# Sixteen loads of V moved from SyncE's queue to ScalarE's

## The chip, the cores and the metric

The kernel runs on one core of one Trainium2 chip. The core has five engines with an instruction stream each: TensorE (PE, matmuls; PEld is its weight load), VectorE (DVE), ScalarE (ACT), GpSimd (POOL) and SyncE (SP, which computes nothing and issues transfers). They meet only at semaphores. The metric is the device time of one execution in microseconds.

## The reference

One transformer layer over 2048 positions of width 512: a modulated layer norm, attention with 32 heads of 16 in which each position looks at itself and seven earlier positions at a distance of 2, 4, ... 14, the output projection, then a second modulated layer norm and a gated feed-forward of width 1792. Cut to what matters here:

```
qkv = h @ wqkv                                  # h = layernorm(x) * (1 + ca) + sa
idx = pos[:, None] - 2 * arange(8)[None, :]     # masked where idx < 0
logits = einsum('bhsd,bhswd->bhsw', q, k[idx]) * Dh ** -0.5
o = einsum('bhsw,bhswd->bhsd', softmax(logits), v[idx])
x = x + ga * (o @ wo)
out = x + gb * ((silu(h2 @ w1) * (h2 @ w3)) @ w2)   # h2 = layernorm(x) * (1 + cb) + sb
```

## The kernel before

The 2048 positions are sixteen tiles T of 128. Everything is bf16 except the sums in PSUM. Per tile the attention goes like this. VectorE multiplies Q with eight shifted views of K (line 706), TensorE sums the products per head into logits (line 716), VectorE and ScalarE make the softmax (lines 728 to 769, the exponential on line 746). For the values, each tile of V is copied out of PSUM by ScalarE (line 685) and stored to a scratch array in device memory (`v_scratch_dram`, line 689). Later the function `values` loads a shifted window of it back: 128 rows of 6144 bytes, 768 KB, from the tile itself and from the end of the one before it (line 776). That is **the V load**, one per tile. VectorE multiplies what it brought with the attention weights (line 783, below: the V product), TensorE sums (line 792), ScalarE copies the sum out (line 798), a transposing transfer turns it (line 799), TensorE applies the output projection (line 804), VectorE adds the residual (line 808). The feed-forward runs in five groups of tiles: gate and up projections on TensorE (line 820), Silu (line 826) and the copy of the up half (line 830) on ScalarE, their product on VectorE (line 831), the down projection (lines 851 and 863), the residual (line 879), the store of the output (line 881).

Nothing of this order is found at run time. `_build` makes some 1100 operations; a list `ORDER` written out in the file places them in one sequence, and each engine's program is that sequence with the other engines' operations left out. `synchronize` then gives each operation the waits that it needs and that its own engine has not already passed. A transfer is an operation of the engine that issues it: it stands in that engine's program, its waits are waited for there, and everything later in that program stands behind it. Before the change all transfers but the load of `c` are in SyncE's program.

A V load waits for the store of its tile's V (for even tiles also of the tile before; tile 0 for the zero padding instead) and for the V product that last used its buffer. There are three buffers: two of `vsh`, and `vshx`, which lies over weights that are dead by then. `SLOTS` names the buffer for each load.

The places of the V loads in `ORDER` beside ScalarE's operations, with the times of the profiled execution (us from the start of the span; the last instruction of ScalarE ahead of the load in the list, the first behind it):

| tile | buffer | SyncE issues | lands | ScalarE ahead | ScalarE behind | V product starts |
|---|---|---|---|---|---|---|
| 0 | vsh 0 | 30.20 | 35.36 | L665 26.30-26.71 | L612 28.76 | 43.99 |
| 1 | vsh 1 | 30.85 | 37.26 | L612 29.44-30.21 | L524 30.10 | 41.79 |
| 2 | vsh 0 | 51.14 | 56.93 | L685 48.79-49.41 | L665 49.27 | 65.80 |
| 3 | vsh 1 | 53.47 | 61.95 | L664 57.64-58.24 | L685 58.84 | 62.76 |
| 4 | vsh 1 | 65.07 | 70.12 | L826 66.92-67.30 | L665 67.20 | 79.71 |
| 5 | vsh 0 | 73.81 | 78.99 | L826 78.47-78.86 | L830 79.00 | 83.58 |
| 6 | vshx | 76.64 | 82.33 | L569 83.09-83.91 | L798 83.81 | 96.31 |
| 7 | vsh 0 | 87.01 | 92.09 | L612 87.13-87.73 | L826 87.58 | 93.39 |
| 9 | vsh 1 | 90.08 | 95.18 | L826 95.96-96.34 | (tile 12's load) | 132.31 |
| 12 | vsh 0 | 95.71 | 100.32 | (tile 9's load) | L830 96.25 | 161.74 |
| 8 | vshx | 120.68 | 126.16 | L826 129.88-130.48 | L826 130.37 | 130.10 |
| 10 | vshx | 132.42 | 137.25 | L830 131.80-132.44 | L830 133.56 | 139.72 |
| 11 | vsh 1 | 134.62 | 140.98 | L798 136.41-137.03 | L830 137.67 | 142.26 |
| 15 | vshx | 142.04 | 146.73 | L826 142.93-143.53 | L830 143.72 | 171.96 |
| 13 | vsh 1 | 148.41 | 152.72 | L830 150.88-151.48 | L830 151.35 | 164.55 |
| 14 | vsh 0 | 164.04 | 169.88 | L798 175.75-176.34 | L798 176.24 | 175.82 |

Of the kernel before, what the change touches and what calls it, by code (L numbers as in the profile page):

```python
# [260 lines left out]
def c_act(n):  # L261
    return 66 + n * 107 // 128


def c_dve(n):
    return 60 + n * 137 // 128
# [12 lines left out]
def _build(p, A_x, A_wqkv, A_wo, B_w1, B_w3, B_w2, c, w_mod, out):  # L279
# [68 lines left out]
    def bank(v):  # L348
        return PALL[:, v.at * 512:(v.at + 1) * 512]
# [52 lines left out]
    vkpad, vzrow, vvpad = Val("kpad"), Val("zrow"), Val("vpad")  # L402
# [18 lines left out]
    for i in range(3):  # L421
        for half in range(2):
            p.dma(wqkv[:, half::2, i * D:(i + 1) * D], wqkv_view[:, half::2, i * D:(i + 1) * D], ("load", 3 + i), (256, 1024),
                  w=[vwq[i][half]])
# [22 lines left out]
    for g in range(NG):  # L447
# [8 lines left out]
         r=[vthc, vcT], w=[vc4])  # L456
# [3 lines left out]
         r=[vc4, vident] + wm_hold, w=[vpc])  # L460
# [169 lines left out]
    vq, vk, vv_dram = {}, {}, {}  # L630
# [142 lines left out]
    def values(T, i, val):  # L773

        vv = Val("vsh", vshpool)
        p.dma(lambda: vv.at[:], bass.AP(v_dram, (PAD + T * P - 2) * D, [[4 * D, 32], [-4 * D, 4], [1, 6 * D]]), ("vl", T), (128, 6144),
              r=[vv_dram[T]] + ([] if T % 2 else [vv_dram[T - 1]] if T else [vvpad]), w=[vv], cost=640, again=True)
        vr = Val("pr", pqpool)

        def av(e):  # L780
            a_w = bass.AP(val.at, i * 8 * H, [[2 * 8 * H, P], [H, 8], [0, DH], [1, H]])
            v_w = bass.AP(vv.at, 2 * D, [[6 * D, P], [-2 * D, 2], [D, 4], [1, D]])
            return e.tensor_tensor(bass.AP(vr.at, 0, [[8 * D, P], [1, 8 * D]]), v_w, a_w, ALU.mult)  # L783

        avs[T] = p.op("dve", av, C_PQ, ("av", T), r=[val, vv], w=[vr], lock=True)
        vo, vt = Val("ps_o", psum), Val("ot", otpool)

        def acc(e):
            b = bank(vo)
            for wf in range(2):  # L790
                for c in range(4):
                    ins = e.matmul(b[32 * c:32 * c + 32, :], ind[:], bass.AP(vr.at, (4 * wf + c) * D, [[8 * D, P], [1, D]]),  # L792
                                   start=(wf == 0), stop=(wf == 1), tile_position=(0, 32 * c))
            return ins

        p.op("pe", acc, C_RED, ("ac", T), r=[vr, vind], w=[vo], tiled=True)
        va = Val("oa", oapool)
        p.op("act", lambda e: e.activation(va.at[:], bank(vo), ACT.Copy), c_act(512), ("ac", T), r=[vo], w=[va])  # L798
        p.dma(lambda: vt.at[:], lambda: va.at[:], ("ac", T), (128, 1024), r=[va], w=[vt], cost=1250, transpose=True)
        vy = Val("ps_y", psum)  # L800

        def wop(e):
            for ft in range(KT):
                ins = e.matmul(bank(vy), vt.at[:, ft, :], wo[:, ft, :], start=(ft == 0), stop=(ft == KT - 1))  # L804
            return ins

        p.op("pe", wop, 4 * MM, ("wo", T), r=[vt, vsc_wo], w=[vy])
        p.op("dve", lambda e: e.scalar_tensor_tensor(x_sb[:, T, :], bank(vy), 1.0, x_sb[:, T, :], op0=ALU.mult, op1=ALU.add,  # L808
                                                     accum_out=sx[:, T, :]), c_dve(512) + 12, ("rs", T), r=[vy], w=[vx[T], vsx[T]])
# [103 lines left out]
    for groups in BLOCKS:  # L913
        vls = [logits(Ts) for Ts in groups]
        ves = [shift(Ts, vl) for Ts, vl in zip(groups, vls)]
        for Ts, vl, ve, vx_ in zip(groups, vls, ves, exps(groups, vls, ves)):
            val = softmax(Ts, vl, ve, vx_)
            for i, T in enumerate(Ts):
                values(T, i, val)
# [102 lines left out]
```

## Time and profile before

| | us, or as said |
|---|---|
| time of the runs shown, median (lowest, highest) | 246.49 (245.53, 247.45) |
| the profiled execution's own time | 247.83 |
| its span, first to last instruction | 245.8 |
| granted TensorE clock, mean (no time, share of full) | 0.992 |
| moved by SyncE's queue (q1) | 35.94 MB |
| moved by ScalarE's queue (q10) | the 1 KB load of `c` |

Busy is the time in which an engine executes an instruction; issuing a transfer is not counted. The idle time that the views show before an instruction is put down to whatever released it last. A row of the timeline is: start, duration, engine (SPq and ACTq are the issuing parts of SyncE and ScalarE), line, operation, tiles, how many were merged, and in brackets the idle time before it with its releaser. All transfers carry line 127, that of the helper that issues them.

### The profile page before, as it was taken

To read this page: it belongs to the slowest core of one execution; us is meant where nothing else is said; L and a number is where in the kernel's file an instruction comes from. 1 tells how busy PE (TensorE), PEld (TensorE's weight loads), DVE (VectorE), ACT (ScalarE), POOL (GpSimd) and SP (SyncE) were. 2 spreads that over 40 slices of the span, in tenths; PEclk is the share of its full clock that TensorE was granted. 3 is DMA by queue.
4 is the path that set the end of the run, shared out by engine and by line. 5 is a ranking of instruction groups with operands and counts; after the bars stand their busy time and mean duration, and the time that the engine had idled before them with its cause. 6 is when DMAs were issued, how large, how long until landed. Compare 5 with 4: busy or idle time off the path is not lost.

```text
span 245.8 us, 4285 instructions
## 1 busy us (share of the span) xinstructions
PE 234.7 (96%) x1669; PEld 120.1 (49%) x1669; DVE 173.1 (70%) x305; ACT 154.5 (63%) x305; POOL 20.9 (8%) x52
## 2 busy tenths in 40 slices
PE   7799999999998999899899999999999999999994
PEld 2557555444556666545443434443334444444473
DVE  4567999999897899988999996592942322142621
ACT  2168677797998889764587879456556944351200
POOL 4124111002000200031000001100000110000000
PEclk9799999999999999999999999999999999999999
DMA  6999979879958687703332964443031120010002
GB/s 191 345 311 350 303 273 207 188 185 350 299 131 249 217 214 244 173 21 67 87 126 59 266 164 154 72 109 121 21 87 23 43 65 16 9 57 9 3 19 67
DMA packets 39348, 36.21 MB, mean 147 GB/s; under 512 B 18832, under 2 KB 36256, under 8 KB 39328
## 3 DMA queue, kind: packets, MB, share of 16 engines
q1 hardware_dynamic: 39320, 35.94, 51.6%
q8 instruction: 13, 0.21, 0.4%
q14 instruction: 7, 0.06, 0.1%
q10 hardware_dynamic: 8, 0.00, 0.0%
HBM read 27.53 MB, written 4.21 MB: 129 GB/s over the span
## 4 chain that ended last, share of the span: by engine, by line
PE 48%; DMA 3%; ACT 2%; DVE 0%; issue 0%; DVEq 0%
PE pall L820 30%; PE pall L863 12%; PE pall L804 3%; DMA sb_h<-sb_xn 2%; PE pall L792 2%; DMA out_dram<-sb_o 1%; ACT sb_h L589 1%; PE pall L851 1%; DVE sb_o L879 0%; ACT sb_xn L569 0%; PE pall L716 0%; ACT sb_hh L830 0%; DVEq L225 0%
## 5 line engine op out<-in xcount | busy, mean ns | idle before, releaser
L820 PE MATMUL pall<-sb_h,sb_w 128*128 128x512 bf16 (+1 forms) x560 | 101.5, 337 | 1.4 <-ACT sb_h L589 1.0
L820 PEld LDWEIGHTS pall<-sb_h,sb_w 128*128 128x128 bf16 x560 | 51.5, 98 | 50.4 <-ACT sb_sg L826 5.8
L826 ACT ACTIVATE sb_sg<-pall 128x512 bf16<-128x512 f32 (+1 forms) x70 | 34.0, 514 | 26.5 <-PE pall L820 25.9
L863 PE MATMUL pall<-sb_w,sb_hh 128*128 128x512 bf16 x196 | 43.5, 379 | 0.0
L706 DVE TENSOR_TENSOR sb_pq<-sb_q,sb_kT 128x4096 bf16<-128x4096 bf16 x16 | 36.3, 2282 | 0.0
L656 PE MATMUL pall<-sb_h,sb_wqkv 128*128 128x512 bf16 (+1 forms) x160 | 33.0, 350 | 1.0 <-DVE sb_h L619 0.6
L830 ACT ACTIVATE sb_hh<-pall 128x256 bf16<-128x256 f32 (+1 forms) x56 | 26.3, 493 | 9.6 <-PE pall L820 9.0
L863 PEld LDWEIGHTS pall<-sb_w,sb_hh 128*128 128x128 bf16 x196 | 19.0, 98 | 22.8 <-DVE sb_hh L831 0.3
L783 DVE TENSOR_TENSOR sb_pq<-sb_vsh,sb_al 128x4096 bf16<-128x4096 bf16 x12 | 27.3, 2286 | 1.1 <-PE pall L716 0.8
L831 DVE TENSOR_TENSOR sb_hh<-sb_sg,sb_hh 128x256 bf16<-128x256 bf16 (+1 forms) x56 | 18.5, 352 | 11.7 <-ACT sb_hh L830 11.3
L879 DVE TENSOR_TENSOR sb_o<-pall,sb_x 128x512 bf16<-128x512 f32 (+1 forms) x18 | 11.0, 628 | 16.8 <-PE pall L863 12.4
L656 PEld LDWEIGHTS pall<-sb_h,sb_wqkv 128*128 128x128 bf16 x160 | 15.0, 102 | 15.2 <-ACT sb_v L685 1.2
L834 DVE TENSOR_TENSOR sb_hh<-sb_sg,pall 128x512 bf16<-128x512 bf16 x14 | 8.9, 684 | 15.3 <-PE pall L820 13.2
L804 PE MATMUL pall<-sb_wo,sb_ot 128*128 128x512 bf16 x64 | 16.0, 379 | 2.6 <-DMA sb_ot<-sb_oa 2.5
L589 ACT ACTIVATE sb_h<-sb_h,sb_modc 128x512 bf16<-128x512 bf16 x16 | 11.7, 811 | 10.0 <-DMA sb_h<-sb_xn 10.0
L612 ACT ACTIVATE sb_h<-pall,sb_modc 128x256 bf16<-128x256 bf16 (+1 forms) x22 | 12.5, 649 | 8.4 <-DVE sb_modc L487 6.1
L564 POOL TENSOR_SCALAR sb_rs<-sb_var 128x2 f32<-128x2 f32 x8 | 4.0, 500 | 147.7 <-ACT sb_xn L558 147.7
L675 PE MATMUL pall<-sb_wqkv,sb_h 128*128 128x512 bf16 x64 | 16.5, 379 | 0.0
L808 DVE SCALAR_TENSOR_TENSOR sb_x<-pall,sb_x 128x512 bf16<-128x512 f32 x16 | 10.9, 688 | 8.0 <-PE pall L804 7.9
L569 ACT ACTIVATE sb_xn<-sb_x,sb_nb,sb_rs 128x512 bf16<-128x512 bf16 x16 | 12.5, 809 | 4.4 <-DVE sb_nb L566 4.4
L665 ACT ACTIVATE sb_kT<-pall 128x512 bf16<-128x512 f32 (+1 forms) x20 | 9.9, 521 | 4.9 <-PE pall L656 4.7
L558 ACT ACTIVATE sb_xn<-sb_x,sb_nm 128x512 bf16<-128x512 bf16 x16 | 11.4, 713 | 2.3 <-DVE sb_nm L554 2.2
(79 smaller groups left out, 217.1 us busy)
## 6 DMA issues: line engine op xcount, KB each, us to landing
sb_vsh<-v_scratch_dram SPq DMA_DIRECT2D x12, 768.0 KB, 5.2
sb_w<-in_B_w_dram SPq DMA_DIRECT2D x6, 512.0 KB, 6.7
sb_vshx<-v_scratch_dram SPq DMA_DIRECT2D x4, 768.0 KB, 5.2
sb_x<-in_A_x_dram SPq DMA_DIRECT2D x18, 128.0 KB, 5.1
sb_w<-in_B_w_dram SPq DMA_DIRECT2D x6, 384.0 KB, 8.2
v_scratch_dram<-sb_v SPq DMA_DIRECT2D x16, 128.0 KB, 5.6
out_dram<-sb_o SPq DMA_DIRECT2D x14, 128.0 KB
sb_wqkv<-in_A_wqkv_dram SPq DMA_DIRECT2D x6, 256.0 KB, 6.4
```

Of the source, the lines that this page charges most:

```text
L569: p.op("act", lambda e, vn=vn, T=T: e.activation(vn.at[:], x_sb[:, T, :], ACT.Identity, bias=nb[:, T, :], scale=rs[:, NT + T, :]), c_act(5 ...
L589: return e.activation(vh.at[:, ft, 0:n * P], vh.at[:, ft, 0:n * P], ACT.Identity, bias=modc[:, 8 * which + ft:8 * which + ft + 1], scale=m ...
L656: ins = e.matmul(bank(vp)[:, 0:n], wqkv[:, t, kind * D + ft * P:kind * D + (ft + 1) * P], vh.at[:, t, 0:n], start=(t == ORDER[0]), stop=(t ...
L675: ins = e.matmul(bank(vp), vh.at[:, t, tt * P:(tt + 1) * P], wqkv[:, t, 2 * D:3 * D], start=(t == ORDER[0]), stop=(t == ORDER[-1]))
L706: return e.tensor_tensor(vp.at[:], in0, in1, ALU.mult)
L783: return e.tensor_tensor(bass.AP(vr.at, 0, [[8 * D, P], [1, 8 * D]]), v_w, a_w, ALU.mult)
L804: ins = e.matmul(bank(vy), vt.at[:, ft, :], wo[:, ft, :], start=(ft == 0), stop=(ft == KT - 1))
L820: ins = e.matmul(bank(vp)[:, 0:n], wt[:, t, fi * P:(fi + 1) * P], vh.at[:, t, 0:n], start=(t == 0), stop=(t == KT - 1))
L826: p.op("act", lambda e: e.activation(vt.at[:, 0:n], bank(vgp)[:, 0:n], ACT.Silu), c_act(n), k, r=[vgp], w=[vt], table="silu")
L830: p.op("act", lambda e: e.activation(vh_.at[:, 0:n], bank(vup)[:, 0:n], ACT.Copy), c_act(n), k, r=[vup], w=[vh_])
L831: p.op("dve", lambda e: e.tensor_tensor(vh_.at[:, 0:n], vt.at[:, 0:n], vh_.at[:, 0:n], ALU.mult), 60 + n * 69 // 128, k, r=[vt], w=[vh_], ...
L863: ins = e.matmul(bank(vz), vhh[fi].at[:, tt * P:(tt + 1) * P], w2[:, fi, :], start=(fi == 0), stop=(fi == NF - 1))
```

## The change

The V load gets the argument `eng="act"`. The helper `dma` hands it to `op`, which puts the operation into that engine's program. `ORDER` and `SLOTS` stay as they are, so each V load takes the place in ScalarE's program that the table above shows, with the waits that ScalarE has not passed by then. The stores of V, the transposing transfers, the weights, x and the output stay with SyncE, in their order.

```diff
@@ -774,7 +774,7 @@
         vv = Val("vsh", vshpool)
         p.dma(lambda: vv.at[:], bass.AP(v_dram, (PAD + T * P - 2) * D, [[4 * D, 32], [-4 * D, 4], [1, 6 * D]]), ("vl", T), (128, 6144),
-              r=[vv_dram[T]] + ([] if T % 2 else [vv_dram[T - 1]] if T else [vvpad]), w=[vv], cost=640, again=True)
+              r=[vv_dram[T]] + ([] if T % 2 else [vv_dram[T - 1]] if T else [vvpad]), w=[vv], cost=640, again=True, eng="act")
```

## The prediction

> **What bounds the kernel now.** I read the page's busy times first, then the chain of work that ended last in order of time.
>
> ```profile
> span 245.8 us, 4285 instructions
> PE 234.7 (96%) x1669; PEld 120.1 (49%) x1669; DVE 173.1 (70%) x305; ACT 154.5 (63%) x305; POOL 20.9 (8%) x52
> ```
> ```profile
> 121.05 14.21 PE pall L820 x64
> ...
> 205.83 24.17 PE pall L820 x112
> ```
>
> TensorE is busy 96% of the span, and from 121 us to the last tiles the chain runs along its matmuls alone. A wait that TensorE gets is therefore paid in full, and a wait that goes pays only if TensorE stood behind it. So the second question is who waits for V loads now. In the view of waits the V product (L783) is never held by a transfer; the first row below is its only one, for a matmul. The largest of TensorE's waits for transfers is for the transposed attention output, which stays where it is:
>
> ```profile
> DVE sb_pq L783 <- PE pall L716: 0.8, 1, 0.8
> ...
> PE pall L804 <- DMA sb_ot<-sb_oa: 2.5, 3, 1.3
> ```
>
> SyncE, on the other hand, waits for V products before it can issue V loads into used buffers:
>
> ```profile
> SPq L127 <- DVE sb_pq L783: 20.8, 6, 10.5
> ```
>
> These 20.8 us leave SyncE. Nothing is late because of them: if every wait of TensorE for a transposed tile vanished too, 2.5 us were gained, 1%. So the change has little to win, and the question is what it costs on ScalarE.
>
> **The change part by part.** Per load three things move: the issue itself, the waits ahead of it, and the moment of issue, which becomes ScalarE's place in the list instead of SyncE's.
>
> The issue costs this on SyncE (minimum, median, maximum in ns), and the one transfer that ScalarE issues today costs it the same there:
>
> ```profile
> L127 SPq DMA_DIRECT2D sb_vsh<-v_scratch_dram x12: 518/586/617, 30.2 to 164.0; - x12
> DMA to landing us min/median/max: 4.3/5.2/8.5
> ```
> ```profile
> 0.78 0.55 ACTq L127 DMA_DIRECT2D sb_c<-in_c_dram  x1
> ```
>
> Sixteen times 0.59 us are 9.4 us of ScalarE's queue. How much of that the engine feels depends on whether its queue gets ahead of it. The trace shows that it does. The semaphore waits of the activation on L589 start at 112.4, while the activation before it in the program starts only at 113.31:
>
> ```profile
> L225 ACTq EVENT_SEMAPHORE  x2: 17/1406/2795, 112.4 to 112.5; - x2
> ```
> ```profile
> 113.31 0.83 ACT L569 ACTIVATE sb_xn<-sb_x,sb_nb,sb_rs 128x512 bf16<-128x512 bf16 x1
> ```
>
> So I take it that a V load is issued as soon as the activation ahead of it has its semaphores, some 0.5 to 2 us before that activation ends, and that an issue of 0.59 us is hidden wherever ScalarE has an activation running and one queued. That covers tiles 1, 2, 4, 5, 6, 7, 11, 13 and 15; I put 0.2 us on the nine together, with 4.4 us as the upper end (six fully paid at 0.59, two that a short gap follows at 0.4, tile 11 in a gap of 0.65). Tiles 9 and 12 stand back to back, 1.2 us of issue against one short activation: 0.4 us, between 0 and 0.9.
>
> *Tile 0: a wait in front of the projections.* SyncE finishes an issue at 23.62 + 1.96 = 25.58 and then stands until 30.20, when the store of V's first tile has landed. That wait moves to ScalarE:
>
> ```profile
> 23.62 1.96 SPq L127 DMA_DIRECT2D sb_x<-in_A_x_dram  x4
> 30.20 1.25 SPq L127 DMA_DIRECT2D sb_vsh<-v_scratch_dram  x2
> ```
> ```profile
> 26.30 0.41 ACT L665 ACTIVATE sb_kT<-pall 128x256 bf16<-128x256 f32 x1
> 28.76 1.45 ACT L612 ACTIVATE sb_h<-pall,sb_modc 128x512 bf16<-128x512 bf16 x2 [2.05 <-PE pall L604]
> ...
> 32.05 0.59 ACT L664 ACTIVATE sb_q<-pall 128x512 bf16<-128x512 f32 x1
> ```
> ```profile
> 33.20 1.59 PE L716 MATMUL pall<-sb_pq,sb_E 128*32 128x256 bf16 x48
> ```
> ```profile
> 34.56 0.67 DVE L728 TENSOR_REDUCE sb_mx<-pall 128x64 f32<-128x512 f32 x1
> ```
> ```profile
> 30.00:40.00 10.00, 10.00 (x120) 5.33 (x119) 10.00 (x16) 7.84 (x15) 1.85 (x4) 1.00 0.81 270
> ```
>
> Queued behind it on ScalarE are the modulated transposes (L612) and the evacuations of the projections. They start at 30.20 + 0.59 = 30.8 instead of 28.76, 2.0 us late. TensorE's next projections want their banks and their input, the logits of 33.20 come 2.0 us late, and the row maximum of 34.56, which follows their end at once, 1.9 us. In 30 to 40 us TensorE and VectorE are both busy 10.00 of 10, so nothing there gives it back: **1.9 us**.
>
> *Tile 3: a later landing.* Its place on ScalarE is behind the activation of 57.64:
>
> ```profile
> 53.47 0.62 SPq L127 DMA_DIRECT2D sb_vsh<-v_scratch_dram  x1
> ```
> ```profile
> 57.64 0.60 ACT L664 ACTIVATE sb_q<-pall 128x512 bf16<-128x512 f32 x1 [0.48 <-PE pall L656]
> 58.84 0.60 ACT L685 ACTIVATE sb_v<-pall 128x512 bf16<-128x512 f32 x1 [0.60 <-DMA v_scratch_dram<-sb_v]
> ```
> ```profile
> 62.76 2.28 DVE L783 TENSOR_TENSOR sb_pq<-sb_vsh,sb_al 128x4096 bf16<-128x4096 bf16 x1
> 65.80 2.29 DVE L783 TENSOR_TENSOR sb_pq<-sb_vsh,sb_al 128x4096 bf16<-128x4096 bf16 x1 [0.75 <-PE pall L716]
> ```
>
> The issue itself fits into the 0.60 us before 58.84. With the median of 5.2 us it lands at 57.7 + 5.2 = 62.9, with the longest of 8.5 us at 66.2; the product starts at 62.76, and the idle 0.75 us behind it absorb as much. That is 0 to 2.7 us; I take 0.3, nearer the median, since the 8.5 us was a load queued behind weights in SyncE's own queue.
>
> *Tile 8: the place is too late.* SyncE issued this load 10 us before its product; on ScalarE it stands behind the first of the two activations of 129.88.
>
> ```profile
> 120.68 0.56 SPq L127 DMA_DIRECT2D sb_vshx<-v_scratch_dram  x1
> ```
> ```profile
> L225 ACTq EVENT_SEMAPHORE  x1: 17/17/17, 129.2 to 129.2; - x1
> ```
> ```profile
> 127.48 0.58 ACT L746 ACTIVATE pall<-pall 128x512 f32<-128x512 f32 x1
> ...
> 129.88 1.08 ACT L826 ACTIVATE sb_sg<-pall 128x512 bf16<-128x512 f32 x2
> ...
> 133.56 0.60 ACT L830 ACTIVATE sb_hh<-pall 128x512 bf16<-128x512 f32 x1 [1.13 <-PE pall L820]
> ```
> ```profile
> 130.10 2.29 DVE L783 TENSOR_TENSOR sb_pq<-sb_vshx,sb_al 128x4096 bf16<-128x4096 bf16 x1
> 132.31 2.28 DVE L783 TENSOR_TENSOR sb_pq<-sb_vsh,sb_al 128x4096 bf16<-128x4096 bf16 x1
> 134.51 0.75 DVE L831 TENSOR_TENSOR sb_hh<-sb_sg,sb_hh 128x512 bf16<-128x512 bf16 x2
> ```
> ```profile
> 135.18 1.05 PE L792 MATMUL pall<-sb_pq,sb_ind 128*32 128x512 bf16 x16
> ```
>
> The semaphore row is the wait of the second of those activations, so the queue has passed the V load's place by 129.2; it cannot be there much before the exponential starts at 127.48, with three instructions then waiting in front. I take 127.9. Landing 5.0 us later, 132.9, makes the product 2.8 us late (1.5 to 4.8 over issue from 127.3 to 129.2 and landings of 4.3 to 5.7). Two chains carry this to TensorE. VectorE's next product, of 132.31, ends 2.8 us late, and the sums of 135.18 follow it directly, with some 0.5 us between. And tile 10's load, next in ScalarE's queue, waits for tile 8's product to leave the shared buffer: ScalarE stands until 130.10 + 2.8 + 2.29 = 135.2, issues, and the copy of 133.56, for which TensorE needs the bank, starts at 135.8, 2.2 us late. Tile 10's and 11's products come after the shift and are not late a second time. **2.4 us** (1.0 to 4.3).
>
> *Tile 14: the place is too late again.* It stands between the two copies of 175.75:
>
> ```profile
> 164.04 0.58 SPq L127 DMA_DIRECT2D sb_vsh<-v_scratch_dram  x1
> ```
> ```profile
> 175.75 1.09 ACT L798 ACTIVATE sb_oa<-pall 128x512 bf16<-128x512 f32 x2 [0.34 <-PE pall L792]
> ...
> 181.04 0.60 ACT L826 ACTIVATE sb_sg<-pall 128x512 bf16<-128x512 f32 x1 [0.27 <-PE pall L820]
> ```
> ```profile
> 175.82 2.29 DVE L783 TENSOR_TENSOR sb_pq<-sb_vsh,sb_al 128x4096 bf16<-128x4096 bf16 x1 [0.30 <-PE pall L792]
> 179.08 0.43 DVE L831 TENSOR_TENSOR sb_hh<-sb_sg,sb_hh 128x512 bf16<-128x512 bf16 x1 [0.97 <-ACT sb_hh L830]
> ```
> ```profile
> 180.84 1.89 PE L804 MATMUL pall<-sb_wo,sb_ot 128*128 128x512 bf16 x8
> ```
>
> The first copy waited for a matmul, so the queue is not ahead here. Issue at 175.8, landing 5.2 us later at 181.0, product until 183.3, the gate product of 179.08 until 183.7; it frees the buffer that the Silu of 181.04 writes, which ends at 184.3 and frees the bank of the second output projection. That one started half-way through the row of 180.84, at 181.7: about **2.5 us**, 1.7 to 3.2 over landings of 4.3 to 5.8.
>
> On SyncE, behind the longest of the waits (10.5 us, for tile 10's load) stood a store of the output, which nothing awaits; on TensorE and VectorE no instruction changes. The sum is 1.9 + 0.3 + 0.4 + 2.4 + 2.5 + 0.2 = 7.7 us. The profiled execution took 247.83 us by its own time (span 245.8), so it would take 255.5. It lies 1.3 us above the median of the runs, 246.49; on the median the sum gives 254.2. With its bounds not all at one end the case spans 251 to 258.
>
> **The rivals.**
>
> *The queue gets further ahead, and the change is not slower by more than 2%.* If a V load need not wait until the activations ahead of it have their semaphores, tile 14's is issued while its copy still waits for TensorE. Landing by 178.3 costs nothing, by the 2.5 us just found, so it decides whether the issue comes before 173.1; tile 8's would be issued by 127.3 and cost 1.2 us. Left are 1.9 + 1.2 + 0.3, together 3.4: 249.9 us. For it speaks the lead at 112.4. Against it, the wait row of 129.2 came just after a VectorE result. [...]
>
> *The issue waits until ScalarE has finished what is ahead of it.* Then nothing is hidden: 4.4 for the nine, 0.9 for the pair, 0.8 for tile 3, 1.9 for tile 0; tile 8 issued at 130.48 lands 5.4 us late, 4.9 us for TensorE; tile 14 issued at 176.3 costs 3.1. Sum 16.0: 262.5 us. The lead in the trace speaks against it, but that row is a wait and no transfer.
>
> *The freed queue of SyncE makes it faster.* It would have to bring the transposed tiles sooner; their waits hold 2.5 us in all, and no V load is queued just ahead of them: at best 244, and only if ScalarE's waits cost nothing. [...]
>
> **How the numbers follow.** What a measurement of this kernel can tell from no change is about 2%, 4.9 us: 241.6 to 251.4. The forecast has 0.58, the early issue 0.22, the late issue 0.14, the gain 0.03; 0.03 is for slowdowns that I did not find. The forecast lies above 251.4 but for its lowest twentieth, the late issue wholly, the early issue mostly below. Slower: 0.55 + 0.14 + 0.03 = 0.72; faster by over 2%: 0.02; within: 0.26. The range takes in the early issue's value and the forecast's upper end and part of the way to the late issue: 249.3 to 259.8.
>
> **What would show it.** ScalarE idle before L612 near 28.8 until 30.8, with the idle put to a transfer; V products near 130 and 176 waiting for `sb_vshx` and `sb_vsh` transfers, 2 to 4 and 5 us; ScalarE idle until tile 8's product ends; issues on ACTq of 0.5 to 0.6 us that overlap running activations. If the V loads of tiles 8 and 14 are issued by 126 and 173, or only after the activation ahead has ended, the rule for the issue was wrong; if the products wait but the chain at the end is not longer, the cover was.

## The result

| | time, us (median; lowest to highest) | runs | against the kernel before |
|---|---|---|---|
| before | 246.49; 245.53 to 247.45 | 2 | |
| V loads on ScalarE | 261.98; 261.38 to 262.57 | 2 | 1.063, 95% interval 1.042 to 1.083 |

15.5 us were added where the prediction said 7.7, and the time lies outside its range. The profiled execution of the changed kernel took 262.57 us (span 260.5, 14.7 more than before), at the same mean granted clock, 0.992. Times of one kernel spread (256.03 to 261.26 us in e0_again below, at mean clocks of 1.000 and 0.985 to 0.987), because stretches at half clock, which are shown below, came and went from run to run, and the ratios leave out a run that is over 1.5% above the fastest of its kernel.

The page of the changed kernel: ScalarE and VectorE do the same work as before, TensorE's share falls from 96% to 91%, and two slices of the granted clock in the middle are no longer full.

```profile
PE 236.9 (91%) x1669; PEld 121.1 (46%) x1669; DVE 173.1 (66%) x305; ACT 154.7 (59%) x305; POOL 20.5 (8%) x52
...
PEclk9999999999999988999999999999999999999999
...
q10 hardware_dynamic: 2312, 12.58, 14.7%
```

The view of waits (who waited for whom: total, times, longest one) has four rows that were small or absent before. The first was 2.5 us; it is the one that the prediction called "the largest of TensorE's waits for transfers" and left out of the sum:

```profile
PE pall L804 <- DMA sb_ot<-sb_oa: 8.4, 5, 2.5
DVE sb_pq L783 <- DMA sb_vsh<-v_scratch_dram: 7.6, 3, 5.0
ACT sb_h L612 <- DMA v_scratch_dram<-sb_v: 5.8, 1, 5.8
...
DVE sb_pq L783 <- DMA sb_vshx<-v_scratch_dram: 1.9, 1, 1.9
```

**Where the time came in.** Taking the start of the same TensorE instruction in both records and noting where the difference jumps gives this account:

| place in the changed kernel's record | us added | what TensorE waited for |
|---|---|---|
| start, to 13 us | -1.2 | nothing; before was at half clock here |
| projection at 32.82 | 3.5 | ScalarE, which waited for the store of V's first tile |
| output projection of tile 1, 56.20 | 2.8 | transposed attention output |
| tile 5 | 0.8 | its V load landing late |
| output projection of tile 4, 95.42 | 2.4 | transposed attention output |
| 96.0 to 99.4 | 1.6 | nothing: half clock |
| tiles 9 and 12 | 0.5 | the pair of issues |
| between 57 and 92 and between 108 and 133 | 0.7 | several small ones |
| tile 8 | 1.3 | its V load landing late, and tile 10's load behind it |
| output projections of tiles 13 and 15, near 195 | 2.4 | transposed output, and tile 14's late load |

The sum is 14.8 us, against 14.7 between the spans. Some half of it, 7.6 us, stands in four rows to which the prediction gave nothing: the output projections of tiles 1 and 4, the landing of tile 5's load, the half clock.

**ScalarE at the first load.** The timeline of ScalarE and its issuing part (start, duration, engine, line, operation; in brackets the idle time before it and its releaser), and of TensorE:

```profile
30.67 0.60 ACTq L127 DMA_DIRECT2D sb_vsh<-v_scratch_dram  x1
31.32 0.78 ACT L612 ACTIVATE sb_h<-pall,sb_modc 128x512 bf16<-128x512 bf16 x1 [5.81 <-DMA v_scratch_dram<-sb_v]
31.37 0.55 ACTq L127 DMA_DIRECT2D sb_vsh<-v_scratch_dram  x1
32.00 0.77 ACT L612 ACTIVATE sb_h<-pall,sb_modc 128x512 bf16<-128x512 bf16 x1
```
```profile
32.82 1.04 PE L656 MATMUL pall<-sb_h,sb_wqkv 128*128 128x512 bf16 x4 [3.35 <-ACT sb_h L612]
```

The wait is where it was forecast, and it ends where it was forecast (30.7 plus the issue). But it is 5.8 us long, where the times of the forecast make 4.1 (26.7 to 30.8): ScalarE was through with its work ahead of it at 25.5. The second load, whose place is behind the activation of 32.00, was issued at 31.37: the issue ran 0.63 us ahead of the engine here.

**The transposed output.** Tile 2's load stands on ScalarE just ahead of the moment at which SyncE issues the transposing transfers of tiles 1 and 0:

```profile
50.21 0.52 ACTq L127 DMA_DIRECT2D sb_vsh<-v_scratch_dram  x1
```
```profile
50.39 2.61 SPq L127 DMA_TRANSPOSE sb_ot<-sb_oa  x2
```
```profile
56.20 1.04 PE L804 MATMUL pall<-sb_wo,sb_ot 128*128 128x512 bf16 x4 [2.49 <-DMA sb_ot<-sb_oa]
```

The view of transfers says what these two took from issue to landing (median of the two): the first row is from the record of before, the second from that of after.

```profile
sb_ot<-sb_oa SPq DMA_TRANSPOSE x2, 2.3
```
```profile
sb_ot<-sb_oa SPq DMA_TRANSPOSE x2, 5.4
```

And the packets of the 16 transfer engines in two stretches of the changed record, 51.6 to 54.4 and 54.4 to 56.0 us:

```profile
DMA packets 100, 0.61 MB, mean 219 GB/s; under 512 B 0, under 2 KB 0, under 8 KB 100
...
q10 hardware_dynamic: 100, 0.61, 83.8%
```
```profile
DMA packets 1114, 0.40 MB, mean 248 GB/s; under 512 B 1085, under 2 KB 1093, under 8 KB 1114
...
q1 hardware_dynamic: 1077, 0.27, 98.9%
```

The transposing transfers' packets are the small ones: 1085 of the 1114 of the second stretch are under 512 bytes. Issued at 50.4 and 51.7, these transfers have none in the first stretch: there only the 6144-byte rows of the V load run, 0.61 MB in 2.8 us, at 83.8% of the engines' time. When most of these are through, the small packets come in a dense block, SyncE's queue at 98.9%. So the two queues did not share the engines evenly in these stretches: of these transfers the one begun first was finished first.

### The profile page after: what moved, and what is told of

The parts are those of the page before. It is cut to its first block, busy times and chain, and to the rows that moved or that the text cites. A ratio compares the mean times of both kernels' runs of the same rounds, so it can differ in the third digit from the quotient of the medians.

```text
span 260.5 us, 4279 instructions
## 1 busy us (share of the span) xinstructions
PE 236.9 (91%) x1669; PEld 121.1 (46%) x1669; DVE 173.1 (66%) x305; ACT 154.7 (59%) x305; POOL 20.5 (8%) x52
## 3 DMA queue, kind: packets, MB, share of 16 engines
q10 hardware_dynamic: 2312, 12.58, 14.7%
## 4 chain that ended last, share of the span: by engine, by line
PE 40%; DMA 6%; ACT 3%; DVE 2%; issue 1%; ACTq 0%; DVEq 0%
PE pall L820 23%; PE pall L863 12%; PE pall L804 2%; DMA sb_vsh<-v_scratch_dram 2%; DMA sb_h<-sb_xn 2%; DMA sb_vshx<-v_scratch_dram 2%; DMA out_dram<-sb_o 1%; PE pall L792 1%; ACT sb_h L589 1%; DVE sb_pq L783 1%; PE pall L851 1%; ACT L746 0%; ACT sb_sg L826 0%; ACT sb_hh L830 0%; DVE sb_o L879 0%
## 5 line engine op out<-in xcount | busy, mean ns | idle before, releaser
L820 PE MATMUL pall<-sb_h,sb_w 128*128 128x512 bf16 (+1 forms) x560 | 103.1, 340 | 3.4 <-ACT sb_hh L830 1.5
L820 PEld LDWEIGHTS pall<-sb_h,sb_w 128*128 128x128 bf16 x560 | 52.5, 99 | 53.3 <-ACT sb_sg L826 5.5
L656 PE MATMUL pall<-sb_h,sb_wqkv 128*128 128x512 bf16 (+1 forms) x160 | 31.9, 341 | 3.9 <-ACT sb_h L612 3.7
L783 DVE TENSOR_TENSOR sb_pq<-sb_vsh,sb_al 128x4096 bf16<-128x4096 bf16 x12 | 27.3, 2287 | 7.6 <-DMA sb_vsh<-v_scratch_dram 7.6
L612 ACT ACTIVATE sb_h<-pall,sb_modc 128x256 bf16<-128x256 bf16 (+1 forms) x22 | 12.5, 651 | 11.9 <-DVE sb_modc L487 5.9
L834 DVE TENSOR_TENSOR sb_hh<-sb_sg,pall 128x512 bf16<-128x512 bf16 x14 | 8.9, 684 | 15.3 <-PE pall L820 13.2
L804 PEld LDWEIGHTS pall<-sb_wo,sb_ot 128*128 128x128 bf16 x64 | 5.4, 97 | 18.6 <-issue 6.7
L664 ACT ACTIVATE sb_q<-pall 128x512 bf16<-128x512 f32 (+1 forms) x20 | 9.7, 519 | 6.1 <-PE pall L656 6.1
## 6 DMA issues: line engine op xcount, KB each, us to landing
sb_wqkv<-in_A_wqkv_dram SPq DMA_DIRECT2D x6, 256.0 KB, 5.3
```

The lines of the kernel that those rows point to most:

```text
L656: ins = e.matmul(bank(vp)[:, 0:n], wqkv[:, t, kind * D + ft * P:kind * D + (ft + 1) * P], vh.at[:, t, 0:n], start=(t == ORDER[0]), stop=(t ...
L820: ins = e.matmul(bank(vp)[:, 0:n], wt[:, t, fi * P:(fi + 1) * P], vh.at[:, t, 0:n], start=(t == 0), stop=(t == KT - 1))
```

## The experiments

In kernels that have one line more, the lines of the views are larger by one (L783 is L784 there). The times are medians of all runs of a kernel. Each comparison is with runs of the kernel before on the same chip: 244.90 us (e0 to e3), 245.62 (e4 to e7), 245.14 (g), 246.72 (h).

| run | V loads on ScalarE | us | against before (95%) |
|---|---|---|---|
| e0_again | all | 260.22 (256.03 to 261.26) | 1.063, of the medians; 1.045 for the run of 256.03 |
| e1 | all but 0, 1 | 252.75 | 1.031 (1.026 to 1.035) |
| e2 | all but 2, 6 | 261.81 | 1.066 (1.057 to 1.074) |
| e3 | all but 8, 14 | 256.40 | 1.043 (1.035 to 1.050) |
| e4 | none, two places moved | 245.91 | 1.002 (0.999 to 1.004) |
| e5 | all, eleven at other places | 250.39 | 1.014 (1.008 to 1.021) |
| e6 | all, three in halves | 263.68 | 1.072 (1.067 to 1.078) |
| e7 | 4, 9 to 13, 15 | 245.38 | 0.999 (0.996 to 1.001) |
| g1 | e7's and 0, 1 | 253.47 | 1.033 (1.026 to 1.039) |
| g2 | e7's and 2, 6 | 251.19 | 1.023 (1.017 to 1.029) |
| g3 | e7's and 8, 14 | 251.04 | 1.019 (1.010 to 1.028) |
| g4 | all, idle time of TensorE filled | 263.47 | 1.067 (1.055 to 1.080) |
| h1 | all, nine at other places | 247.24 | 1.004 (1.000 to 1.007) |
| h2 | all but 2 to 7 | 256.35 | 1.041 (1.037 to 1.046) |
| h3 | e7's and 3, 5, 7 | 251.09 | 1.019 (1.011 to 1.026) |

For e1 to e3, e7, g1 to g3, h2 and h3 the edit to the kernel before is this, with the tiles of the table:

```diff
+ACT_V = (2, 3, 4, 5, 6, 7, 8, 9, 10, 11, 12, 13, 14, 15)
...
-              r=[...], w=[vv], cost=640, again=True)
+              r=[...], w=[vv], cost=640, again=True, eng="act" if T in ACT_V else "sp")
```

### The changed kernel again, and its groups taken back

> The changed kernel once more, for a tight interval. All theories: 261 to 263 us, 1.06 times the kernel before (246.49 us). What the trace should repeat, by the theory of the landings: ScalarE idle some 5.8 us before the activation of L612 near 31 us; the transposed attention output of tiles 1 and 4 landing 5.0 to 5.8 us after its issue instead of 2.3 to 2.4; a stretch of about 3 us at half the granted clock near 96 us. If the stretch at half clock or the late landings are missing in this profile at the same time, they were an accident of the first record.

260.22 us, and the waits repeat: ScalarE idle 4.6 us for the store of V ahead of L612, the transposed output of tiles 1 and 0 at 4.9 us (median), tile 4's at 5.6. The stretch at half clock did not repeat at 96 us; such stretches came at the start and behind the wait for tile 0. Of the four runs three had a mean clock of 0.985 to 0.987 and took 260.18 to 261.26 us, and the fourth had 1.000 and took 256.03. So in these runs some 4 us of the 15 are clock, and 11 are waits. The share differs from record to record: in the account of the first one, half clock adds 1.6 us and its absence at the start takes 1.2 off.

> V loads of tiles 0 and 1 back on SyncE, the other fourteen on ScalarE. Theory of the landings: ScalarE no longer waits 5.8 us for the store of V's first tile before L612, so the shift of TensorE near 30 us (3.5 us, net 2.3 against the clock of the start) goes: 2.3 to 3.5 us less than the changed kernel, 258.5 to 259.7 us. Rival, ScalarE pays for each issue (0.59 us): two issues less, 1.2 us, 260.8 us. Rival, two queues cost as such: 14 of 16 loads still there, 260 us and the wait at L612 is not what matters.

252.75 us, 7.5 less than e0_again: more than any theory gave. The store of V holds ScalarE no longer, and the clock stays full in three of the four runs (0.999 to 1.000). But the 7.5 us are not all the cost of tiles 0 and 1. Between the two profiled records 2.4 us are gained ahead of the place, where e0_again happened to be at half clock; 2.5 us are gained at the wait, 1.7 at half clock behind it and 1.5 at tile 4's output projection. At full clock the kernels differ by 3.5 us (256.03, one run, and a median of 252.52), nearly twice the 1.9 us of the prediction.

> V loads of tiles 2 and 6 back on SyncE, the other fourteen on ScalarE. Theory of the landings: the transposing transfers of the attention output of tiles 1 and 4 are no longer behind a load of 768 KB in the transfer engines and land 2.3 to 2.4 us after their issue again; TensorE's waits at L804 near 53 and 92 us go (2.8 and 2.4 us), and with the second of them the stretch at half clock (1.5 us): 6.7 us less, 255.3 us (256.8 if the stretch has another cause). Rival, each issue on ScalarE costs 0.59 us: 1.2 us less, 260.8 us. Rival, two queues cost as such: 2 of 16 parts of 15.5 us, 1.9 us less, 260 us.

261.81 us: nothing gained, though the mechanism did what was expected. TensorE's waits at the output projection fell from 8.4 to 1.8 us, and the transfers of tiles 1 and 0 landed after 2.3 us. Something took all of it back. The timeline has it:

```profile
70.99 4.49 DVE L784 TENSOR_TENSOR sb_pq<-sb_vsh,sb_al 128x4096 bf16<-128x4096 bf16 x2 [3.76 <-DMA sb_vsh<-v_scratch_dram]
```
```profile
73.88 0.60 ACT L666 ACTIVATE sb_kT<-pall 128x512 bf16<-128x512 f32 x1 [1.97 <-DVE sb_pq L784]
```

Tile 3's load, issued on ScalarE at 62.04, now finds ahead of it the weights and x that SyncE issued behind tile 2's load, and lands 8.9 us later. The packets from 62.0 to 62.6 us are all SyncE's, 207 of the 231 between 512 bytes and 2 KB:

```profile
DMA packets 231, 0.21 MB, mean 353 GB/s; under 512 B 24, under 2 KB 231, under 8 KB 231
...
q1 hardware_dynamic: 231, 0.21, 104.6%
```

Tile 14's load in the changed kernel, with no packet of any queue between its issue and its first row, had that row 1.3 us after the issue (188.28 to 189.60) and landed after 4.8 us. Why the rows of SyncE's queue held up tile 3's load for so long stays open.

The product of tile 3 is 3.8 us late, and tile 4's load, which wants the same buffer, holds up ScalarE until that product ends, in front of an evacuation for TensorE.

> V loads of tiles 8 and 14 back on SyncE, the other fourteen on ScalarE. Theory of the landings: the products of tiles 8 and 14 are no longer late, and the transposed attention output of tile 13 is not behind tile 14's load: 1.3 and 2.4 us less, 258.3 us. The prediction on record put 2.4 and 2.5 us on them: 257.1 us. Rival, each issue on ScalarE costs 0.59 us: 1.2 us less, 260.8 us. Rival, two queues cost as such: 1.9 us less, 260 us.

256.40 us, 3.8 less than e0_again. The clock of these runs was lower (0.978 to 0.993), so the times alone would not settle it; the profiled records do. Against e0_again's TensorE gains 1.1 us at tile 8 and 2.4 us at the output projections near 195, 3.4 together, close to the 3.7 of the theory of the landings; the prediction's 4.9 was too high. The reverse, g3 against e7 below, shows 1.5 and 2.2 at the same places.

### The order without the queue

```diff
 ORDER = [
 ...
-    ... 272, 404, 405, ... 438, 422,
+    ... 272, 404, 422, 405, ... 438,
 ...
-    ... 345, 478, 668, ... 707, 454,
+    ... 345, 668, ... 707, 478, 454,
```

(422 and 478 are the V loads of tiles 2 and 6, 405 and 454 the transposing transfers of tiles 1 and 4; all on SyncE.)

> The kernel before, every transfer in SyncE's queue; only the places of the V loads of tiles 2 and 6 in the order are moved, to directly ahead of the transposing transfers of the attention output of tiles 1 and 4. Theory of the landings (a transfer issued just behind a load of 768 KB lands late, whichever queue it is in): TensorE waits 2.4 to 2.8 us longer at L804 at both places, 5 us together, up to 6.6 if a stretch at half clock follows the second: 251.5 to 253 us. Rival, two queues contend and one queue does not: 246.5 us.

1.002, no difference: the expectation of 5 us was wrong. But the experiment did not put the load where the theory needs it. SyncE issues the load as soon as it gets there and only then waits for the output to be transposed, so tile 2's load went 1.1 us ahead of the transposing transfers and tile 6's 7 us ahead:

```profile
45.09 0.60 SPq L127 DMA_DIRECT2D sb_vsh<-v_scratch_dram  x1
46.18 2.57 SPq L127 DMA_TRANSPOSE sb_ot<-sb_oa  x2
```
```profile
sb_ot<-sb_oa SPq DMA_TRANSPOSE x2, 3.8
```

With that lead the transposed output still lands after 3.8 us instead of 2.3, in one and the same queue. TensorE comes 1.0 us later through tile 1's output projection than in e7's record, and later stages give most of that back. What the second queue added in the changed kernel is a worse moment: on SyncE tile 2's load was issued 3.2 us behind the first of these two transposing transfers (51.14 and 47.97), on ScalarE 0.2 us ahead of it (50.21 and 50.39).

### All sixteen at better places

```diff
 ORDER = [
 ...
-    ... 225, 258, 394, 247, ... 14, 401, 235, ...
+    ... 225, 258, 247, ... 14, 235, ... 267, 394, 401, 215, ...
```

(394 and 401 are the loads of tiles 0 and 1; likewise for those of tiles 2, 3, 5, 6, 8, 9, 11, 12 and 14. The expectations of e5 and h1 name tile 7, but the load that moved is tile 11's.)

> All sixteen V loads on ScalarE, eleven of them at other places of the order: tiles 0 and 1 behind the projections that tile 0's wait held up, tiles 2, 6, 7 and 14 away from the transposing transfers of the attention output, tiles 3, 5, 8 and 12 with 9 and 14 earlier or later so that they land in time. Theory of the landings: with no landing late and no transposing transfer behind a load, ScalarE's issues cost next to nothing: 245 to 248 us, the kernel before. Rival, each issue on ScalarE costs up to 0.59 us: 250 to 256 us. Rival, two queues cost as such: 256 to 262 us.

250.39 us. Transposed output lands as in the kernel before (TensorE waits 1.0 us for it, 2.5 there), and no V product waits. What is left is one new wait that these places made: the loads of tiles 8, 9 and 12 stand back to back, 2.3 MB from 114.5 us on, and SyncE's stores of the output behind them come too late for VectorE, which needs their buffer:

```profile
124.85 0.69 DVE L879 TENSOR_TENSOR sb_o<-pall,sb_x 128x512 bf16<-128x512 f32 x1 [4.58 <-DMA out_dram<-sb_o]
```

The next kernel puts tiles 9 and 12 back to the change's places, and tiles 0 and 1 one and three instructions of ScalarE later.

> All sixteen V loads on ScalarE, nine of them at other places of the order than in the changed kernel: tiles 0 and 1 behind the evacuations of the projections that the first logits need, tiles 2, 6, 7 and 14 away from the transposing transfers of the attention output, tile 8 ten places earlier, tiles 3 and 5 earlier; tiles 9 and 12 at the change's places. If the changed kernel lost its time only by what its loads were issued behind and ahead of, nothing is left: 244.5 to 247 us, 0.995 to 1.007 of the kernel before. If sixteen issues on ScalarE or a second queue cost by themselves: 250 us or more. In the trace: ScalarE not idle for a store of V, transposed output 2.3 to 5 us behind its issue as in the kernel before, V products not waiting for their loads.

247.24 us, 1.004. Sixteen issues on ScalarE, the second queue and the relieved SyncE together cost 0.35%, 0.9 us, and 1.7 us at the end of the interval. The rest of the change's cost, some 6% of the medians, is places: the same sixteen loads, of which nine stand elsewhere in the list. In h1's view of waits there is no row in which a V product waits for its load or ScalarE for a transfer of V, and the output projection waits 2.8 us for transposed tiles (2.5 before):

```profile
PE pall L804 <- DMA sb_ot<-sb_oa: 2.8, 3, 1.4
```

### A load in two halves

```diff
-        p.dma(lambda: vv.at[:], bass.AP(v_dram, ... [1, 6 * D]]), ("vl", T), ...
+        half = T in (2, 6, 14)
+        ...
+        p.dma(*part(n0, 6), ("vl", T), ... eng="act",
+              pre=[part(0, n0)] if half else ())
```

> The changed kernel with the loads of tiles 2, 6 and 14 each issued as two transfers, of the left and the right half of the columns (rows of 3072 bytes instead of 6144). If a transfer engine finishes its share of a transfer that it has begun before it turns to another queue, the transposed output of tile 1 lands after one half at best, some 1.5 us sooner: 4.2 us behind its issue instead of 5.8, and that of tile 4 likewise; TensorE gains up to 1.5 us at each of the three places, less the three added issues (0.5 us each where they are not hidden): 258 to 261 us. If the engines serve transfers in the order of their issue whatever their size, the transposed output still lands 5 to 5.8 us behind its issue: 262 us, up to 263.5 with the issues.

263.68 us: neither gain nor the unchanged landing at every place. The packets of three stretches of this record (54.8 to 55.9, 56.1 to 56.9 and 57.1 to 57.5 us) show what the engines did at tile 2:

```profile
DMA packets 84, 0.26 MB, mean 235 GB/s; under 512 B 0, under 2 KB 0, under 8 KB 84
```
```profile
DMA packets 496, 0.21 MB, mean 258 GB/s; under 512 B 467, under 2 KB 467, under 8 KB 496
```
```profile
DMA packets 52, 0.16 MB, mean 392 GB/s; under 512 B 1, under 2 KB 1, under 8 KB 52
```

First one half alone, then small packets beside the tail of it, then again the rows of the load: in this record 457 packets of SyncE's queue ran from 56.1 to 56.9 us, between the two halves, as the first theory had it. But the transfers were also issued in this order (the first half at 53.27, tile 1's transposing transfer at 53.45, the second half at 53.82), so the record does not tell a turn from service in the order of issue, and the time is that of the second theory. Half of the small packets of tiles 1 and 0 fit in between, and the rest stands behind the second half. Tile 1's output lands after 5.4 us instead of 5.8, tile 4's after 3.3 instead of 5.6, tile 15's after 7.3 instead of 4.7: there both halves were issued ahead of it. (This profiled run was the slowest of the five, 268.71 us.)

### The parts added to loads that cost nothing

> The kernel before with seven V loads on ScalarE, those of tiles 4, 9, 10, 11, 12, 13 and 15, at the places that the change gives them, where no landing was late and no transposing transfer followed closely. Theory of the landings: the issues are hidden behind running activations, 246.5 to 247.5 us (0.6 us for the pair of tiles 9 and 12). Rival, each issue on ScalarE costs up to 0.59 us: 249.5 to 250.6 us. Rival, two queues cost as such: 7 of 16 parts of 15.5 us, 253 us.

0.999, with an interval from 0.4% less to 0.1% more: seven issues of 0.52 to 0.59 us on ScalarE cost nothing that can be measured. The price of 0.59 us for each issue falls, and with it the rival that the issue waits for the engine. The activation ahead of tile 9's load in the list is the second one here; the issue came before it, beside the first:

```profile
92.67 0.38 ACT L827 ACTIVATE sb_sg<-pall 128x256 bf16<-128x256 f32 x1
92.81 0.52 ACTq L127 DMA_DIRECT2D sb_vsh<-v_scratch_dram  x1
92.95 0.38 ACT L827 ACTIVATE sb_sg<-pall 128x256 bf16<-128x256 f32 x1
```

> The seven V loads that cost nothing on ScalarE (tiles 4, 9, 10, 11, 12, 13, 15) and those of tiles 0 and 1; seven stay on SyncE. If the wait on ScalarE for the store of V's first tile is the largest single cost, it alone gives 4 to 7.5 us over the kernel before (about 245.5 us in these runs): 249.5 to 253 us; 4 us where the granted clock stays full behind TensorE's idle time, 7.5 us where it is halved. By the prediction on record, 1.9 us: 247.4 us. Rival, the cost of tiles 0 and 1 comes only with all sixteen: 245.5 us.

253.47 us, 8.3 over the kernel before. ScalarE waits 7.0 us here and TensorE 4.5, and then the granted clock is 0.50 in a row of the windows view that is 4 us long (after the clock stand the transfers' share and rate):

```profile
31.90 0.78 ACT L613 ACTIVATE sb_h<-pall,sb_modc 128x512 bf16<-128x512 bf16 x1 [7.00 <-DMA v_scratch_dram<-sb_v]
```
```profile
33.40 1.89 PE L657 MATMUL pall<-sb_h,sb_wqkv 128*128 128x512 bf16 x4 [4.54 <-ACT sb_h L613]
```
```profile
34.00:38.00 4.00, 4.00 (x11) 1.32 (x9) 0.00 (x0) 1.76 (x3) 0.00 (x0) 0.50 0.81 306
```

> The seven that cost nothing and tiles 2 and 6. Taking these two back from the changed kernel gave nothing, though the waits for the transposed output went, because a load of tile 3, a wait of ScalarE for a store of V and the load of tile 5 were late in their place. If the transfer engines are what is shared, adding them alone to a kernel without other waits brings the waits at L804 back: 2.5 us at tile 1's and 1.0 to 2.4 us at tile 4's, 3.5 to 4.9 us: 249 to 250.4 us. Rival, they cost nothing: 245.5 us.

251.19 us, 6.0 over before and above the 3.5 to 4.9 expected. The waits at the output projection come back; the first row is of g2, the second of e7:

```profile
PE pall L805 <- DMA sb_ot<-sb_oa: 7.9, 5, 2.6
```
```profile
PE pall L805 <- DMA sb_ot<-sb_oa: 1.9, 3, 0.9
```

Against e7's record TensorE loses 2.2 us at tile 1's output projection, 2.5 at tile 4's, and 1.5 at half clock behind the first. So these two places do hold up the end, where nothing else does.

> The seven that cost nothing and tiles 8 and 14, whose places in ScalarE's list come too late. Theory: 1.0 us for tile 8's product and tile 10's wait behind it, 2.2 us at the end for tile 14's product and tile 13's transposed output: 248.7 us. By the prediction on record 2.4 and 2.5 us: 250.4 us. If the slack of the other places hides them: 245.5 us.

251.04 us, 5.9 over before, with a wide spread (248.62 to 253.37). The profiled run is the lowest: 248.62, the 248.7 that the waits alone gave. The others had more, two of them with a lower clock (0.990 and 0.986); without the highest the median is 250.26, 5.1 over.

> V loads of tiles 2 to 7 back on SyncE, the other ten on ScalarE. Taking back tiles 2 and 6 alone gave nothing, with tile 3's product 3.8 us and tile 5's 1.9 us late and ScalarE waiting for a store of V ahead of tile 4's load. If these three took back what the two had given, they go here, and of the 15 us of the changed kernel about 5.6 us go (2.2 and 2.5 at the output projections of tiles 1 and 4, 1.0 for late products): 254.5 us, 1.037 to 1.04 of the kernel before. If the two places never held the end up: 260 us, 1.06.

256.35 us, 1.041, where 1.037 to 1.04 was expected. With tiles 3 to 7 on SyncE as well, taking back tiles 2 and 6 does help: tile 3's product no longer waits. Against e0_again's record TensorE gains 2.2 and 2.5 us at the two output projections, and keeps them. So the puzzle of e2 was the loads behind them, and not that the two places were harmless. (The expectations of g2 and h2 name a store of V that ScalarE waits for; the row of L666 under e2 shows that ahead of tile 4's load it was tile 3's product.)

> The seven V loads that cost nothing and those of tiles 3, 5 and 7; tiles 0, 1, 2, 6, 8 and 14 on SyncE. The prediction on record put 0.3 us on tile 3 and nothing on tiles 5 and 7. In the changed kernel tile 3's product was 1.7 us late and tile 5's 0.9 us. Theory: 0 to 1.5 us over the kernel before, 1.00 to 1.006. Rival, ScalarE pays for issues: three more at 0.59 us, 1.007.

251.09 us, 4.4 over before: far from the 0 to 1.5 expected. Tile 3's place on ScalarE is 4 us later than SyncE's was, and in these 4 us SyncE, no longer held by V loads, has issued its bulk. The load lands 8.6 us after its issue, as long as on SyncE (8.5), but from a later start; the product and tile 4's load follow as in e2, and tile 5's product waits 2.0 us in the same way:

```profile
64.20 4.49 DVE L784 TENSOR_TENSOR sb_pq<-sb_vsh,sb_al 128x4096 bf16<-128x4096 bf16 x2 [3.54 <-DMA sb_vsh<-v_scratch_dram]
```
```profile
67.10 0.60 ACT L666 ACTIVATE sb_kT<-pall 128x512 bf16<-128x512 f32 x1 [1.48 <-DVE sb_pq L784]
```

Alone the four groups cost 8.3, 6.0, 5.9 and 4.4 us, 24.6 together; with all sixteen moved it is 15.3 (260.22 less 244.90), 11.1 at full clock. The waits overlap: where TensorE is late already, a load has more time, and with tile 2's load out of SyncE's queue tile 3's lands after 6.0 us and not 8.6.

### TensorE's idle time filled

```diff
+FILL = ((("q", 9), 13), (("wo", 1), 9), (("wo", 4), 10))
...
+        def fill(e, vp=vp, count=count):
+            for _ in range(count):
+                ins = e.matmul(bank(vp), ones[:, 0:P], ones[:], start=True, stop=True)
+            return ins
+        p.op("pe", fill, count * MM, ("fill", key), r=[vc], hold=[vp])
```

> The changed kernel with matrix products of no use put into three of TensorE's idle stretches: 13 ahead of the projection that waits for ScalarE near 30 us, 9 and 10 ahead of the output projections of tiles 1 and 4 (0.216 us each at full clock: 2.8, 1.9 and 2.2 us of stretches of 3.3, 2.5 and 2.8 us). They write the bank that the waiting product overwrites, and nothing reads them. If the granted clock is halved because TensorE stood idle, no stretch at half clock follows these three places, and 1.7 to 3.4 us of each such stretch are saved: 256 us, the time of the one run of the changed kernel at clock 1.00. If the halving has another cause, it stays: 260 to 262 us.

263.47 us, inconclusive. At the two output projections the fillers ran and no half clock followed (1.00 from 56 to 60 and from 97 to 101 us), but the changed kernel itself had one at only one of the two, in one of two records. At tile 0 the fillers failed: the bank that they write is freed by the same late activation, so they waited with everything else, and then ran at half clock themselves (0.50 from 34 to 39 us):

```profile
34.16 4.45 PE L935 MATMUL pall<-sb_ones 128*128 128x512 bf16 x10 [4.05 <-ACT sb_h L613]
```

By the author's reading of the program every bank of PSUM holds a result there that waits for ScalarE, so there was none to fill without a wait. What share of the cost is clock is known only from e0_again's one run at full clock and from the stretches in the records.

## Why the prediction failed

The sign was right, and where the prediction named a place the loss was there (tile 3 apart); the size was not, because it gave no cost to other places that held half of the loss. Step by step:

**"The largest of TensorE's waits for transfers is for the transposed attention output, which stays where it is".** This is the step that failed: these transfers were held to be untouched, and the sum had no term for them. The transfer stays in its place in SyncE's program, but a load that leaves the program meets it in the 16 engines that both queues use (ScalarE's took 83.8% of them from 51.6 to 54.4 us, SyncE's 98.9% from 54.4 to 56.0). Tile 2's load was issued 0.2 us ahead of it, tile 6's 1.3 us ahead of tile 4's, tile 14's 0.6 us ahead of tile 15's. The first two cost 2.8 and 2.4 us in the record, with 1.6 at half clock behind the second, and 6.0 us alone (g2). Without these and without tile 5's 0.8 the account comes to 7.2 us, near the 7.7 of the sum; but that closeness is partly luck, since tile 0 came out higher than its term and tile 8 lower. The table of places in front of the prediction shows these moments: tile 6's load, issued at 76.64 on SyncE, stood behind ScalarE's activation of 83.09, next to the copy that feeds the transposing transfer of 84.41. They were read for what ScalarE would feel, and not for what else would be issued then.

**Tile 0, 1.9 us.** The right wait, mis-sized: 3.5 us in the record (2.3 net of the 1.2 that this record had gained by then), some 8 with tile 1's load alone (g1). The sum was made against one record, and in that record TensorE had lost its clock early, so it came to this place late. The first two rows are the windows view of before and of after over the same stretch; the others are ScalarE at L612 in before and, in the same place with the same wait, in e7:

```profile
9.40:12.90 3.50, 3.02 (x15) 2.17 (x16) 1.92 (x6) 0.71 (x2) 0.54 (x2) 0.53 1.10 367
```
```profile
9.40:12.90 3.50, 3.31 (x25) 2.42 (x24) 2.35 (x7) 1.53 (x6) 0.94 (x2) 1.00 1.09 362
```
```profile
28.76 1.45 ACT L612 ACTIVATE sb_h<-pall,sb_modc 128x512 bf16<-128x512 bf16 x2 [2.05 <-PE pall L604]
```
```profile
26.48 1.45 ACT L613 ACTIVATE sb_h<-pall,sb_modc 128x512 bf16<-128x512 bf16 x2 [2.05 <-PE pall L605]
```

At full clock ScalarE wants to go on at 26.5 and not at 28.8, while the store of V lands at 30.0 to 31.3 in the records of before, after, e7 and g1, 7.7 to 8.5 us after its issue. The same sum with 26.5 gives 30.8 - 26.5 = 4.3 us. Tiles 0 and 1 cost 8.3 in g1: TensorE is idle for 4.5, and half clock, from 31.6 to 38.4, adds 2.5 behind it.

**Tile 3, 0.3 us (up to 2.7).** The longest landing of 8.5 us was set aside because that load was queued behind weights in SyncE's own queue. But that load was tile 3's own (53.47 to 61.95 in the table of places), and behind SyncE's weights it took as long from ScalarE's queue: 8.6 us in h3, 8.9 in e2. In the changed kernel itself it was 6.0, and a late product of 1.7 us was absorbed. Tile 5, counted as hidden, had its issue hidden but its landing late, 0.8 us.

**Tiles 9 and 12, 0.4 us:** 0.5 in the record. **The hidden issues, 0.2 us:** right; e7 bounds seven issues at 0.3 us, and h1 puts 0.9 on all sixteen with their second queue.

**Tile 8, 2.4 us, and tile 14, 2.5 us.** The mechanisms are the ones named. The product of tile 8 waits 1.9 us and ScalarE then for tile 10's load; that of tile 14 waits 5.0:

```profile
143.07 2.29 DVE L783 TENSOR_TENSOR sb_pq<-sb_vshx,sb_al 128x4096 bf16<-128x4096 bf16 x1 [1.90 <-DMA sb_vshx<-v_scratch_dram]
```
```profile
193.09 2.29 DVE L783 TENSOR_TENSOR sb_pq<-sb_vsh,sb_al 128x4096 bf16<-128x4096 bf16 x1 [5.05 <-DMA sb_vsh<-v_scratch_dram]
```

They cost 1.3 and 2.4 us in the record, and 1.1 and 2.4 by e3's. Tile 14's term holds 1.0 us that belongs to tile 13's transposed output behind its load. (In the view of waits of before, the V product has a second row, 0.3 us for the matmul of L792, beside the one that the prediction calls its only one; it changes nothing.)

**The rivals.** The queue did get ahead of activations that wait: tile 1's load was issued at 31.37, the activation ahead of it ran at 32.00; tile 8's at 138.60, 2.4 us before the activation ahead of it started (140.99). It got no further for tile 14, whose issue came with the start of its copy (188.28), and it saved little. The rival of the late issue named 262.5 us, close to the result by luck, for a reason that e7 refutes: its sum charged the issues, and the time went to landings. The freed queue of SyncE brought nothing: h1, with all sixteen loads in ScalarE's queue, took 247.24 us, 1.004 of the kernel before, and the change itself took 261.98, because it moved moments as well.

## What to carry to other kernels

When a transfer moves to another queue, list what the other queue issues in the next few microseconds, and who waits for that: here a load of 768 KB was in the way of the small urgent transposing transfers from the other queue (5.4 us to landing instead of 2.3) and from their own (3.8 us in e4). A place in a list is a moment only together with the waits around it; here the cost of the change of queue lay in the moments, and the issues were nearly free (0.999 for seven in e7). Before a wait is sized from one record, look whether that record's clock was full up to there.

## What the hardware showed beyond that

Behind idle time of TensorE the granted clock was 0.50 for a stretch in some places and stayed at 1.00 in others. The record of after around the output projection of tile 4, idle from 92.9 to 95.4 us:

```profile
92.00:95.00 3.00, 0.61 (x8) 0.15 (x8) 3.00 (x6) 1.65 (x5) 0.00 (x0) 1.00 1.36 155
95.00:96.00 1.00, 0.58 (x3) 0.32 (x4) 1.00 (x4) 0.60 (x1) 0.00 (x0) 1.00 1.22 394
96.00:99.00 3.00, 3.00 (x15) 1.92 (x13) 0.29 (x2) 0.50 (x2) 0.00 (x0) 0.50 0.60 212
99.00:100.00 1.00, 1.00 (x9) 0.82 (x8) 0.81 (x3) 0.43 (x2) 0.00 (x0) 0.80 0.24 37
```

Half clock lasted 3.4 us and cost 1.6. The longer idle time of 3.35 us ahead of 32.82 in the same record was followed by none (1.00 from 33 to 36 us), and the 4.54 us in g1 by 6.8 us of it, from 31.6 to 38.4, which began while TensorE was still idle. So such a wait cost 3.5 us in one record and over 7 in another, which is part of the reason why runs of one kernel lie between 256.0 and 261.3.

Other records have stretches of the same two lengths: 3.4 us in before (from 9.6), in e0_again (from 9.2 and from 33.1) and in e3 (from 59.0), 6.8 us in e3 (from 31.7). The length of the idle time does not tell by itself where one comes: 2.5 us had one behind them in the record of after and 3.35 us had none, and the one of before at 9.6 stands beside idle times of 0.43 and 0.57 us. What decides it is not shown.
